# Rescheduling the fill, the transposes and the cluster products of an attention and MLP kernel

## Chip, cores, metric

One NeuronCore of a Trainium2 chip. The metric is the device time of one execution in microseconds, median of the timed runs. "Step" below means one 128-key block of one head; batch 0 to 3 are the four batches of the input, with 48 steps each. SBUF and PSUM are the two memories that this kernel's tiles lie in; M0, M1, M2, OB and SA are PSUM tiles of this kernel. A DMA "lands" when its transfer has ended. Lengths of batches and steps are taken from the start of one exponential to the start of another.

## The reference, cut to what matters

```python
B, H, S, D = 4, 8, 768, 64                      # 16 cluster centroids per head
q_assign = argmax(q_n @ c_n.T); k_assign = argmax(k_n @ c_n.T)
mask   = q_assign[..., :, None] == k_assign[..., None, :]
scores = where(mask, q @ k.T / sqrt(D), -1e9)
attn   = softmax(scores) @ v                    # -> x, 3072 x 512
h = x @ w_in                                    # 512 x 2048
g = h + sin(alpha * h)**2 / (alpha + 1e-9)
out = g @ w_out                                 # 2048 x 512
```

The mask is made by 16 one-hot rows that are appended to the 64 rows of q and k: the score of a query and a key of the same cluster gets a constant more.

## The kernel before

Heads go in pairs (4 pairs a batch). For each pair of batches 0 and 1 (but one) TensorE (PE) transposes q and k in four groups g (`prep_T`, three fp32 transposes each, copied out of PSUM by VectorE, DVE), GpSimd (POOL) casts them into `QK` (`prep_cast`), PE multiplies them with the centroids (`prep_asn`, the "cluster product"), DVE makes the one-hot rows in four pieces (`prep_hot`), and four DMAs bring them into `QK` (`prep_move`). Batches 2 and 3 and the end of batch 1 are transposed by DVE and DMA.

```python
def scores(i):          # 2 matmuls, 512 + 256 columns, into one of two score areas
def expo(i):            # ScalarE (ACT): exp of 128x768
def pv(i):              # 6 matmuls of 65 columns; after the 6th block: rec, xs on DVE
    ...
due = {}                # pv of step r is due at r+3 (first of a head) or r+2
for r in range(ASTEPS):
    due.setdefault(r + (3 if r % NJ == 0 else 2), []).append(r)
    ...
for r in range(ASTEPS):
    i = base + r
    scores(i)
    expo(i)
    ...
    for d in due.get(r, []):
        pv(base + d)
    for fn in plan.get(i, []):     # prep_T, prep_asn, prep_hot ... at their steps
        fn()
    if fill and i not in asn_at:
        fill.go(1)                 # one matmul of the batch before's output
```

So step r%6 = 2 has no PV and step r%6 = 3 has two. The fill matmuls exist in batches 1 to 3: they are the last product (`gT @ w_out`) of the batch before, 64 a batch.

```python
def prep(m, s0):
    if m > 1:
        for g in range(4):
            if m != NHP + 3:
                at(s0 + g, lambda g=g: prep_T(m, g))     # four steps running
        at(s0 + 2, lambda: prep_cast(m, 0))
        at(s0 + 4, lambda: prep_cast(m, 1))
    else:
        s0 -= 4                                          # pair 1: transposed before step 0
    at(s0 + 5, lambda: (prep_asn(m), prep_hot(m, 0)))    # whole product in one step
    at(s0 + 6, lambda: (prep_hot(m, 1), prep_hot(m, 2)))
    at(s0 + 7, lambda: (prep_hot(m, 3), prep_move(m)))
    ...
# --- start, before step 0 (cut) ---
head_asn(0, 0, M0)                 # first cluster product; its one-hot rows gate scores(0)
...
head_move(0, 0, [nc.sync, nc.scalar])
load_v(0); load_qk(2)
prep_T(1, 0, M1, "act"); prep_T(1, 1, M2, "act")
head_asn(0, 1, OB)
...
prep_T(1, 2, M0, "dve"); prep_T(1, 3, M1, "dve")
warmup(4)                          # bf16 matmuls on zeros, result unused
# --- end (cut) ---
spare = [SA[0][:, 0:512], SA[0][:, 512:1024], M1, M2]   # banks of the last output tiles
```

The softmax here doesn't subtract the row's maximum and nothing guards it: scores larger than these inputs give would overflow.

## Time and profile before

| | before |
|---|---|
| timed runs | 320.87, 321.02, 321.75 us; median 321.02 |
| the profiled execution | 323.24 us, span 321.43 us |
| first exponential | 14.30 us |
| first to last exponential, batches 0 to 3 | 42.32, 40.70, 40.34, 38.97 us |
| last exponential to end | 49.23 us |

The page of before; the first line has, for each engine, busy us (share of the span) and number of instructions, the second is the chain that ended last by engine:

```profile
PE 307.7 (96%) x2745; PEld 183.5 (57%) x2787; DVE 207.2 (64%) x362; ACT 242.4 (75%) x326; POOL 112.7 (35%) x174
PE 80%; ACT 6%; DVE 6%; POOL 3%; issue 2%; DMA 1%; SPq 0%; ACTq 0%; DVEq 0%; POOLq 0%
```

PE is what bounds it. Ends of matmuls are modelled, so I read starts. The timeline of before, PE alone, around a step without PV in batch 2 (columns: start us, us, engine, line, operation, out<-in, shape, count):

```profile
173.17 0.38 PE L360 MATMUL M<-w_out_bf,gT 128*128 128x512 bf16 x1
173.38 0.38 PE L313 MATMUL S<-QK 80*128 80x512 bf16 x1
173.60 0.27 PE L314 MATMUL S<-QK 80*128 80x256 bf16 x1
173.71 0.38 PE L360 MATMUL M<-w_out_bf,gT 128*128 128x512 bf16 x1
174.10 0.38 PE L313 MATMUL S<-QK 80*128 80x512 bf16 x1
174.43 0.53 PE L328 MATMUL OB<-VX,pT 128*128 128x65 bf16 x12
174.79 0.38 PE L360 MATMUL M<-w_out_bf,gT 128*128 128x512 bf16 x1
175.02 0.38 PE L313 MATMUL S<-QK 80*128 80x512 bf16 x1
```

A fill matmul (L360) holds PE for 0.21 us (173.17 to 173.38). After the one at 173.71 the next scores start 0.39 us later: 0.18 us are a wait for the exponential that still reads the score area (0.81 us long, from 173.24). In the next step, with two PVs (L328, 12 matmuls) and a fill, PE is late: from scores to scores it takes 0.92 us (174.10 to 175.02).

The end, same view; the bracket is idle time before it and what ended it:

```profile
305.20 1.46 PE L360 MATMUL S<-w_out_bf,gT 128*128 128x512 bf16 x6
307.33 3.61 PE L360 MATMUL S<-w_out_bf,gT 128*128 128x512 bf16 x16 [0.67 <-ACT o_sb L373]
```

And the start, same view:

```profile
12.31 1.41 PE L459 MATMUL S<-warm 128*128 128x512 bf16 x3
13.77 0.38 PE L313 MATMUL S<-QK 80*128 80x512 bf16 x1
13.99 0.27 PE L314 MATMUL S<-QK 80*128 80x256 bf16 x1
```

The warm-ups come about 0.42 us apart, twice the 0.21 of a 512-column matmul later: PE ran at half rate up to about 13.51 us, where the trace's clock record begins. The page's clock row reads full speed there all the same; only the start-to-start times show the half rate. (The record of the fourth warm-up is missing from this trace.)

### The profile page before, as it was taken

What the parts mean: (1) busy time and instruction counts of PE and PEld (TensorE: products, weight loads), DVE (VectorE), ACT (ScalarE), POOL (GpSimd) and SP (SyncE); (2) the same over time, 40 slices, a digit from 0 to 9 for tenths busy, and PEclk for the clock granted to TensorE, in tenths of its full rate; (3) what the DMA queues carried; (4) which work ended last, traced back from release to release, by engine and by line L of the source; (5) the groups of instructions that cost most, each with busy time, mean ns of one, the idle gap of its engine ahead of it and who ended that gap; (6) DMA issues with size and microseconds to landing.
All of it is one profiled execution on the core that took longest, in us unless ns stands there. A gap on an engine that the chain in (4) does not pass through costs nothing.

```text
span 321.4 us, 7151 instructions
## 1 busy us (share of the span) xinstructions
PE 307.7 (96%) x2745; PEld 183.5 (57%) x2787; DVE 207.2 (64%) x362; ACT 242.4 (75%) x326; POOL 112.7 (35%) x174
## 2 busy tenths in 40 slices
PE   7999999899999999999999999999999999999995
PEld 3466665555556565555556566555556666555544
DVE  4488877377858676587858776577835222677721
ACT  5388888787679989687678988777678999687300
POOL 5499788407505363970004476520001000000000
PEclk9999999999999999999999999999999999999999
DMA  6566499996725666881034665420011000000031
GB/s 197 162 199 201 129 191 240 217 204 200 254 89 118 159 150 117 262 297 45 0 98 113 157 164 115 115 82 2 0 67 49 33 2 35 0 36 0 0 133 65
DMA packets 26242, 37.74 MB, mean 117 GB/s; under 512 B 3856, under 2 KB 20064, under 8 KB 26208
## 3 DMA queue, kind: packets, MB, share of 16 engines
q0 software_dynamic: 8704, 19.93, 23.8%
q1 hardware_dynamic: 17264, 17.30, 20.2%
q8 instruction: 22, 0.36, 0.5%
q14 instruction: 12, 0.10, 0.1%
q10 hardware_dynamic: 240, 0.06, 0.1%
HBM read 27.30 MB, written 6.29 MB: 105 GB/s over the span
## 4 chain that ended last, share of the span: by engine, by line
PE 80%; ACT 6%; DVE 6%; POOL 3%; issue 2%; DMA 1%; SPq 0%; ACTq 0%; DVEq 0%; POOLq 0%
PE S L389 16%; PE M L360 16%; PE S L313 13%; PE OB L328 9%; PE M L389 7%; PE S L314 5%; PE OB L360 4%; ACT pT L319 4%; PE M L211 3%; PE S L360 2%; DVE gT L409 2%; PE M L143 2%; POOL QK L185 1%; PE M L352 1%; ACT s_sb L400 1%
## 5 line engine op out<-in xcount | busy, mean ns | idle before, releaser
L319 ACT ACTIVATE pT<-S 128x768 bf16<-128x768 f32 x192 | 145.5, 810 | 23.3 <-PE S L314 19.8
L360 PE MATMUL M<-w_out_bf,gT 128*128 128x512 bf16 (+1 forms) x261 | 83.0, 373 | 0.4 <-DVE gT L409 0.2
L313 PE MATMUL S<-QK 80*128 80x512 bf16 x192 | 73.0, 381 | 4.1 <-ACT pT L319 1.6
L389 PEld LDWEIGHTS <-w_in_bf 128*128 128x128 bf16 x512 | 49.6, 98 | 38.2 <-issue 2.1
L328 PEld LDWEIGHTS <-pT 128*128 128x128 bf16 x1152 | 55.8, 97 | 21.9 <-issue 0.8
L389 PE MATMUL S<-xT,w_in_bf 128*128 128x256 bf16 (+1 forms) x345 | 64.8, 325 | 1.5 <-DVE gT L409 0.8
L328 PE MATMUL OB<-VX,pT 128*128 128x65 bf16 x1152 | 60.7, 194 | 0.6 <-DVE xs L340 0.4
L190 POOL TENSOR_SCALAR QK<-T 64x384 bf16<-64x384 f32 x64 | 33.9, 529 | 69.0 <-DMA T<-Tq 65.8
L400 ACT ACTIVATE s_sb<-S,alpha_col 128x768 bf16<-128x768 f32 x44 | 39.3, 900 | 23.8 <-PE S L389 14.5
L360 PEld LDWEIGHTS <-gT 128*128 128x128 bf16 x400 | 39.0, 98 | 26.3 <-issue 1.5
L314 PE MATMUL S<-QK 80*128 80x256 bf16 x192 | 52.0, 271 | 0.0
L409 DVE SCALAR_TENSOR_TENSOR gT<-u_sb,ralpha,S 128x768 bf16<-128x768 bf16 x44 | 44.5, 1014 | 11.5 <-ACT u_sb L405 8.1
L314 PEld LDWEIGHTS <-QK 80*128 80x128 bf16 x192 | 18.9, 98 | 22.0 <-issue 7.4
L185 POOL CAST QK<-T 64x768 bf16<-64x768 f32 x32 | 26.9, 840 | 8.8 <-DVE T L149 4.0
L389 PE MATMUL M<-xT,w_in_bf 128*128 128x256 bf16 (+1 forms) x154 | 29.4, 324 | 0.3
L339 DVE RECIPROCAL rec<-OB 128x6 f32<-128x6 f32 x32 | 6.2, 194 | 36.2 <-PE OB L328 36.1
L407 DVE TENSOR_TENSOR u_sb<-s_sb 128x768 bf16<-128x768 bf16 x40 | 23.4, 586 | 7.9 <-ACT s_sb L400 7.9
L202 POOL CAST VX<-v 128x768 bf16<-128x768 f32 x16 | 14.2, 889 | 38.4 <-PE OB L328 34.2
L409 DVE SCALAR_TENSOR_TENSOR gT<-u_sb,ralpha,M 128x512 bf16<-128x512 bf16 (+1 forms) x40 | 22.8, 611 | 6.2 <-ACT u_sb L405 5.8
L400 ACT ACTIVATE s_sb<-M,alpha_col 128x512 bf16<-128x512 f32 (+1 forms) x40 | 20.9, 573 | 7.3 <-PE M L389 7.3
L360 PE MATMUL OB<-w_out_bf,gT 128*128 128x512 bf16 (+1 forms) x79 | 25.8, 358 | 0.0
L313 PEld LDWEIGHTS <-QK 80*128 80x128 bf16 x192 | 18.7, 97 | 12.0 <-issue 9.6
(81 smaller groups left out, 272.3 us busy)
## 6 DMA issues: line engine op xcount, KB each, us to landing
T<-Tq SPq DMA_DIRECT2D x64, 96.0 KB, 2.3
out_dram<-o_sb SPq DMA_DIRECT2D x23, 256.0 KB, 2.1
v<-in_v_dram POOLq DMA_DIRECT2D x14, 384.0 KB, 4.9
q<-in_q_dram POOLq DMA_DIRECT2D x13, 384.0 KB, 4.4
k<-in_k_dram POOLq DMA_DIRECT2D x13, 384.0 KB, 5.2
w_in_bf<-in_moe_w_in_dram POOLq DMA_DIRECT2D x4, 512.0 KB, 8.3
w_out_bf<-in_moe_w_out_dram POOLq DMA_DIRECT2D x4, 512.0 KB, 11.5
QK<-ohT SPq DMA_DIRECT2D x60, 24.0 KB, 2.8
```

The costliest lines, as they stand in the source:

```text
L185: nc.gpsimd.tensor_copy(out=QK[0:D, m % NQK, h, :, HS * par : HS * par + HS], in_=src)
L190: nc.gpsimd.tensor_scalar(out=QK[0:D, m % NQK, h, t].rearrange("c (n i a) -> c i n a", i=4, a=32)[:, 2 * par : 2 * par + 2], in0=src[:, t] ...
L202: nc.gpsimd.tensor_copy(out=VX[m % NVX][:, :, :, 0:D], in_=st[m]["v32"])
L313: nc.tensor.matmul(out=dst[:, 0:512], lhsT=lhsT, rhs=T[:, 0, 0:512], start=True, stop=True)
L314: nc.tensor.matmul(out=dst[:, 512:S], lhsT=lhsT, rhs=T[:, 0, 512:S], start=True, stop=True)
L319: nc.scalar.activation(out=pT, in_=area(i)[:, 0:S], func=ACTF.Exp, scale=escale)
L328: nc.tensor.matmul(out=o3[:, j, :], lhsT=pT[:, P * j : P * j + P], rhs=VX[m % NVX][:, h, jof(m // NHP, kt), :], start=(kt == 0 and j == 0) ...
L360: nc.tensor.matmul(out=bk[:, lo:hi], lhsT=gT[:, f, P * mt : P * mt + P], rhs=w_out_bf[:, f, lo:hi], start=(f == 0), stop=(f == NF - 1),)
L389: nc.tensor.matmul(out=ar[lo // 512][:, 0 : hi - lo] if isinstance(ar, tuple) else ar[:, lo:hi], lhsT=lhsT, rhs=xT[:, kk, lo:hi], start=(k ...
L400: nc.scalar.activation(out=s_sb[:, lo:hi], in_=src, func=ACTF.Sin, scale=alpha_col[:, f : f + 1])
L407: nc.vector.tensor_tensor(out=u_sb, in0=s_sb, in1=s_sb, op=ALU.mult)
L409: nc.vector.scalar_tensor_tensor(out=gT[:, f, lo:hi], in0=u_sb[:, lo:hi], scalar=ralpha[:, f : f + 1], in1=src, op0=ALU.mult, op1=ALU.add,)
```

## The change

Its intent: give PE in every step of batches 1 to 3 about the same work; in batch 0, put transposes and halves of the cluster product one per step; start the scores of pair 0 before pair 1's last two transpose groups; warm PE earlier; free the end of its bank wait.

```diff
-    def prep_asn(m, bk=None):
+    def prep_asn(m, part=0, parts=1):          # half of the columns each
 ...
+    load_v(0)                                  # earlier: ahead of load_qk(1)
     load_qk(1)
 ...
+    warmup(2)
     head_asn(0, 0, M0)
 ...
-    prep_T(0, 3, SA[1][:, 0:512], "act")
+    prep_T(0, 3, M1, "act")
 ...
-    prep_T(1, 0, M1, "act")
-    prep_T(1, 1, M2, "act")
+    prep_v(0)
     head_asn(0, 1, OB)
 ...
-    prep_v(0)
-    prep_cast(1, 0)
-    prep_T(1, 2, M0, "dve")
-    prep_T(1, 3, M1, "dve")
-    warmup(4)
-    prep_cast(1, 1)
+    prep_T(1, 0, M2, "act")
+    prep_T(1, 1, M0, "act")
     load_v(1)
+    warmup(2)
 ...
+    def pair_steps(m, make, half, cast):
+        for g, i in make:
+            at(i, lambda g=g: prep_T(m, g))
+        for h in range(2):
+            at(cast[h], lambda h=h: prep_cast(m, h))
+        at(half[0], lambda: prep_asn(m, 0, 2))
+        a = half[1]
+        at(a, lambda: (prep_asn(m, 1, 2), prep_hot(m, 0)))
+        at(a + 1, lambda: (prep_hot(m, 1), prep_hot(m, 2)))
+        at(a + 2, lambda: (prep_hot(m, 3), prep_move(m)))
 ...
-    for m, s0 in {1: 0, 2: 4, 3: 12, 4: 20, 5: 28, 6: 36, 7: ASTEPS + 2}.items():
-        prep(m, s0)
+    for m, make, half, cast in (
+        (1, ((2, 0), (3, 1)), (4, 5), (0, 3)),
+        (2, ((0, 2), (1, 6), (2, 7), (3, 8)), (11, 12), (7, 10)),
+        (3, ((0, 10), (1, 13), (2, 14), (3, 17)), (19, 20), (14, 18)),
+        (4, ((0, 18), (1, 22), (2, 23), (3, 24)), (29, 30), (23, 25)),
+        (5, ((0, 25), (1, 26), (2, 31), (3, 32)), (35, 36), (27, 33)),
+        (6, ((0, 34), (1, 37), (2, 38), (3, 41)), (43, 44), (38, 42)),
+    ):
+        pair_steps(m, make, half, cast)
 ...                                            # loads of q, k at fixed steps; alpha at 42; pair 7 by hot_steps
-            if fill and i not in asn_at:
-                fill.go(1)
+            if fill:
+                fill.go((2 if r % NJ == 2 else 0 if r % NJ == 3 else 1) - (i in asn_at))
 ...
-    spare = [SA[0][:, 0:512], SA[0][:, 512:1024], M1, M2]
+    spare = [SA[0][:, 0:512], M1, SA[0][:, 512:1024], M2]
```

More of the change, by code (lines that the diff above doesn't have):

```diff
@@ L202, in prep_v @@
         nc.gpsimd.tensor_copy(out=VX[m % NVX][:, :, :, 0:D], in_=st[m]["v32"])
-    def prep_asn(m, bk=None):
+    def prep_asn(m, part=0, parts=1):
         s = st[m]
         hp = pair_of[m][1]
-        bk = bank() if bk is None else bk
+        if part == 0:
+            s["asn"] = bank()[:, 0:HS]
+        w = HS // parts
         for g in range(4):
             nc.tensor.matmul(
-                out=bk[32 * g : 32 * g + 32, 0:HS],
+                out=s["asn"][32 * g : 32 * g + 32, w * part : w * part + w],
                 lhsT=cnB[:, 2 * hp + g // 2, :],
-                rhs=s["T32"][:, g, :],
+                rhs=s["T32"][:, g, w * part : w * part + w],
                 start=True,
@@ L217, in prep_asn @@
             )
-        s["asn"] = bk[:, 0:HS]
     def head_asn(m, h, bk):
@@ L497 @@
     prep_T(0, 2, SA[0][:, 0:512], "act")
-    prep_T(0, 3, SA[1][:, 0:512], "act")
+    prep_T(0, 3, M1, "act")
     head_move(0, 0, [nc.sync, nc.scalar])
-    load_v(0)
     load_qk(2)
     prep_cast(0, 1)
-    prep_T(1, 0, M1, "act")
-    prep_T(1, 1, M2, "act")
+    prep_v(0)
     head_asn(0, 1, OB)
@@ L532, in hot_steps @@
         at(a + 3, lambda: (prep_hot(m, 3), prep_move(m)))
-    def prep(m, s0):
-        if m > 1:
-            for g in range(4):
-                if m != NHP + 3:
-                    at(s0 + g, lambda g=g: prep_T(m, g))
-            at(s0 + 2, lambda: prep_cast(m, 0))
-            at(s0 + 4, lambda: prep_cast(m, 1))
-        else:
-            s0 -= 4
-        at(s0 + 5, lambda: (prep_asn(m), prep_hot(m, 0)))
-        at(s0 + 6, lambda: (prep_hot(m, 1), prep_hot(m, 2)))
-        at(s0 + 7, lambda: (prep_hot(m, 3), prep_move(m)))
-        asn_at.add(s0 + 5)
+    def pair_steps(m, make, half, cast):
[8 more added lines that the diff above has]
+        at(a + 2, lambda: (prep_hot(m, 3), prep_move(m)))
     def prep_new(m, k0):
@@ L554, in prep_new @@
         hot_steps(m, k0 + 8)
-    for m, s0 in {1: 0, 2: 4, 3: 12, 4: 20, 5: 28, 6: 36, 7: ASTEPS + 2}.items():
-        prep(m, s0)
-        if m == NHP + 3:
-            at(ASTEPS - 8, lambda m=m: load_qk(m, eng=nc.gpsimd))
-        elif m > 2:
-            at(max(0, s0 - 14), lambda m=m: load_qk(m, eng=nc.gpsimd))
+    for m, make, half, cast in (
[6 rows of a table added]
+    ):
+        pair_steps(m, make, half, cast)
+    for h in range(2):
+        at(ASTEPS + 4 + 2 * h, lambda h=h: prep_cast(NHP + 3, h))
+    hot_steps(NHP + 3, ASTEPS + 7)
+    for m, i in {3: 0, 4: 8, 5: 15, 6: 22, 7: 38}.items():
+        at(i, lambda m=m: load_qk(m, eng=nc.gpsimd))
     late = []
@@ L586, in alpha @@
         nc.vector.reciprocal(out=ralpha, in_=ralpha)
-    at(15, alpha)
+    at(42, alpha)
     def load_w_in(n):
```

## The prediction

> **What bounds the kernel now.** TensorE: the page gives PE 96% busy, ACT 75%, DVE 64%; the chain of waits is 80% PE. Busy PE is modelled, so I read start-to-start times in the timeline. An attention step costs PE 0.32 us of scores, 0.195 of PV (6 matmuls) and, from batch 1 on, 0.21 of a fill matmul. Two score areas alternate: scores of step i+2 wait for the exponential of step i (0.81 us), so two steps take at least 1.45 us.
>
> **Fill (batches 1 to 3).** Six steps without one-hot work take 0.73, 0.73, 0.71, 0.91, 0.73, 0.73 us between exponentials. The step without PV has 0.53 us of PE work, and the next scores wait 0.18 us for the exponential (timeline: fill at 173.71, scores at 174.10). Moving one fill there from the step with two PVs makes 0.75 and 0.71: 0.17 us saved per group. Groups with the cluster product (0.8 us) in the no-PV step don't wait and gain nothing. Free groups: 3 + 3 + 6, plus each batch's first (0.21): 2.7 us, all on the chain.
>
> **End.** The first matmul of output tile 3 waits for ACT's copy out of the other half of its PSUM tile: a PE gap of 0.7 us near 307. Its own bank removes it: -0.75.
>
> **Start.** First exponential at 14.30 us; its one-hot rows landed at 11.6, but PE had pair 1's transposes and 4 warm-ups in front. Two transpose groups leave (1.2 us), and head 1's cluster product no longer waits behind pair 1's loads. Two warm-ups in front of the first cluster product delay it by 0.35. First exponential: about 13.1. [...] Net -0.8.
>
> **Batch 0.** First to last exponential: 42.3 us, against 33 at ACT's 0.707 a step. PE work is about 38: transposes 0.36 a group, product 0.8. The new schedule spreads the lumps (steps of 1.4 to 1.6 us). But it takes in two transpose groups of pair 1 (+0.72 PE, +0.9 DVE), and DVE gets nearly full: 36 us of work in 42. Adding up the PE and DVE queues step by step with the trace's durations (this gives 42.3 for before) shows new waits: pair 1's one-hot ends 9.1 us after the first scores, and its moves (0.62 us issue each, 1.8 to 4.4 to landing) end after step 12 wants them, 1 to 2 us lost; the half product at step 35 waits 1 us for a tile on DVE. So 42.9: +0.6 (-1.5 to +2).
>
> **Sum.** 321.0 - 2.7 - 0.75 - 0.8 + 0.6 = 317.3; leaning slightly lower, since the schedule looks tuned: **317.0 us, range 314.3 to 319.5**. Faster by over 2%: 0.11; within: 0.88; slower: 0.01.
>
> **Right or wrong.** Right if no-PV and two-PV steps read about 0.75/0.71 instead of 0.71/0.91; the gap near 307 is gone; the first exponential comes near 13; steps of 1.4 us mostly leave batch 0, but one is long at 11 to 12 (scores waiting for a DMA of one-hot rows) and one near 35. The stretches between batches (31.6 us) should not change.
>
> **What would make it wrong.** [...]no stall at step 12 (1.5 more gained); DVE backlog stalling more of batch 0; fills in the no-PV step delaying the scores behind them.

The sum came to 317.3 us, and the lean made it 317.0. In the start's paragraph a rule for the clock that no run here shows is cut, and with it the term of +0.4 that rested on it: the -0.8 in the sum is -1.2 (14.30 to 13.1) and that +0.4.

## The result

Ratios below are the mean time of one kernel's runs over that of the other's runs of the same rounds, so not quite the ratio of the medians quoted. Executions over 1.5% slower than the fastest of the same kernel are left out of the means.

| | before | after |
|---|---|---|
| median | 321.38 us (320.87 to 321.83, 4 runs) | 319.31 us (318.93 to 319.74, 4 runs) |
| ratio | | 0.9936 (0.9914 to 0.9959) |
| profiled execution, span | 321.43 us | 317.56 us |
| clock record begins | 13.51 us | 6.42 us |
| first exponential | 14.30 us | 12.27 us |
| batch 0 | 42.32 us | 43.51 us |
| batches 1, 2, 3 | 40.70, 40.34, 38.97 us | 40.34, 39.71, 37.79 us |
| last exponential to end | 49.23 us | 48.39 us |

The median fell by 2.07 us where I had said 4.0. The two traces differ by 3.87, which was the first sign that one of them was not typical. The page of after, as above:

```profile
PE 306.6 (97%) x2835; PEld 183.0 (58%) x2835; DVE 205.3 (65%) x362; ACT 241.3 (76%) x326; POOL 111.3 (35%) x174
PE 86%; DVE 7%; ACT 2%; DMA 2%; issue 1%; SPq 0%; DVEq 0%; ACTq 0%
```

The step without PV, PE's timeline of after:

```profile
171.77 0.38 PE L361 MATMUL M<-w_out_bf,gT 128*128 128x512 bf16 x1
171.98 0.38 PE L314 MATMUL S<-QK 80*128 80x512 bf16 x1
172.20 0.27 PE L315 MATMUL S<-QK 80*128 80x256 bf16 x1
172.31 0.59 PE L361 MATMUL M<-w_out_bf,gT 128*128 128x512 bf16 x2
172.75 0.38 PE L314 MATMUL S<-QK 80*128 80x512 bf16 x1
173.07 0.53 PE L329 MATMUL OB<-VX,pT 128*128 128x65 bf16 x12
173.44 0.38 PE L314 MATMUL S<-QK 80*128 80x512 bf16 x1
```

Two fills take 0.44 us from 172.31 to 172.75 and no wait is left; the step with two PVs goes from scores to scores in 0.69 us (172.75 to 173.44). The no-PV step became 0.76 us between exponentials and the two-PV step 0.71; before they were 0.71 and 0.91. The end, same view: the gap is gone.

```profile
304.76 2.32 PE L361 MATMUL M<-w_out_bf,gT 128*128 128x512 bf16 x10
306.92 3.62 PE L361 MATMUL S<-w_out_bf,gT 128*128 128x512 bf16 x16
```

The start, same view: here the scores wait for a DMA of one-hot rows, and the warm-ups before them run at full rate (0.21 us apart).

```profile
9.77 0.59 PE L461 MATMUL S<-warm 128*128 128x512 bf16 x2
11.75 0.38 PE L314 MATMUL S<-QK 80*128 80x512 bf16 x1 [1.39 <-DMA QK<-ohT]
```

Batch 0 is 1.2 us longer, though its lumps went: nine steps over 1.15 us (up to 1.6) are gone, but three new ones came: step 11 with 2.17 us (before 0.94), step 35 with 2.20 us (before 0.74) and step 2 with 1.23 us (before 0.71). These are PE's waits in batch 0 of after (12 to 56 us: us in total, times, longest us; the first line contains the wait of the start):

```profile
PE S L314 <- DMA QK<-ohT: 2.4, 2, 1.4
PE M L213 <- DVE T L149: 0.6, 1, 0.6
PE M L143 <- DMA q<-in_q_dram: 0.4, 1, 0.4
PE OB L329 <- DVE xs L341: 0.2, 1, 0.2
```

Step 11, PE's timeline of after: after the half product of pair 2 PE idles until pair 1's one-hot rows land, planned at step 7 and due at step 12.

```profile
22.16 0.53 PE L213 MATMUL M<-T,cnB 128*32 128x192 f32 x8
23.72 0.38 PE L314 MATMUL S<-QK 80*128 80x512 bf16 x1 [1.03 <-DMA QK<-ohT]
```

Step 35, PE and then DVE in the timeline of after. The product of pair 5 needs all four transposed tiles; the last copy (T, the first of the two in the last line, ended at 45.38) stands in DVE's queue behind one-hot work of pair 4 (oh, ohT).

```profile
44.30 0.53 PE L213 MATMUL M<-T,cnB 128*32 128x192 f32 x6
45.44 0.51 PE L213 MATMUL M<-T,cnB 128*32 128x192 f32 x2 [0.61 <-DVE T L149]
```

```profile
42.51 1.08 DVE L256 TENSOR_TENSOR oh<-asT,amax 128x384 bf16<-128x384 f32 x1
43.51 0.55 DVE L149 TENSOR_SCALAR T<-M 128x384 f32<-128x384 f32 x1
43.98 0.96 DVE L273 STREAM_TRANSPOSE ohT<-oh 128x768 bf16<-128x768 bf16 x1
44.87 0.98 DVE L149 TENSOR_SCALAR T<-M 128x384 f32<-128x384 f32 x2
```

### The profile page after: what moved, and what is told of

Same layout as the page of the kernel before. It is cut to its first block, busy times and chain, and to the rows that moved or that the text cites. A ratio compares the mean times of both kernels' runs of the same rounds, so it can differ in the third digit from the quotient of the medians.

```text
span 317.6 us, 7292 instructions
## 1 busy us (share of the span) xinstructions
PE 306.6 (97%) x2835; PEld 183.0 (58%) x2835; DVE 205.3 (65%) x362; ACT 241.3 (76%) x326; POOL 111.3 (35%) x174
## 4 chain that ended last, share of the span: by engine, by line
PE 86%; DVE 7%; ACT 2%; DMA 2%; issue 1%; SPq 0%; DVEq 0%; ACTq 0%
PE M L361 18%; PE S L390 16%; PE S L314 12%; PE OB L329 10%; PE M L390 8%; PE S L315 6%; PE OB L361 5%; PE M L213 4%; PE S L361 2%; DVE gT L410 2%; PE M L143 2%; PE M L353 1%; ACT s_sb L401 1%; DMA q<-in_q_dram 1%; DVE u_sb L408 1%
## 5 line engine op out<-in xcount | busy, mean ns | idle before, releaser
L361 PE MATMUL M<-w_out_bf,gT 128*128 128x512 bf16 (+1 forms) x288 | 90.7, 373 | 0.3 <-DVE gT L410 0.3
L390 PE MATMUL S<-xT,w_in_bf 128*128 128x512 bf16 x352 | 65.2, 326 | 1.0 <-DVE gT L410 0.8
L390 PE MATMUL M<-xT,w_in_bf 128*128 128x512 bf16 (+1 forms) x160 | 29.9, 326 | 0.0
L202 POOL CAST VX<-v 128x768 bf16<-128x768 f32 x16 | 13.5, 844 | 34.3 <-PE OB L329 33.4
```

The lines of the kernel that those rows point to most:

```text
L202: nc.gpsimd.tensor_copy(out=VX[m % NVX][:, :, :, 0:D], in_=st[m]["v32"])
L361: nc.tensor.matmul(out=bk[:, lo:hi], lhsT=gT[:, f, P * mt : P * mt + P], rhs=w_out_bf[:, f, lo:hi], start=(f == 0), stop=(f == NF - 1),)
L390: nc.tensor.matmul(out=ar[lo // 512][:, 0 : hi - lo] if isinstance(ar, tuple) else ar[:, lo:hi], lhsT=lhsT, rhs=xT[:, kk, lo:hi], start=(k ...
```

## The experiments

Sixteen kernels ran, in four groups; each group shared eleven runs of before on its chip (medians 321.66, 321.44, 321.44 and 321.33 us). All results were correct.

### 1. Is the profile of before typical? (before_again, before_third)

No edit. Theory A: the profiled execution was one with a late clock; rival B: its start is typical.

> The kernel before, unchanged. Theory A: the profiled execution of before was not typical: its clock was granted only at 13.5 us (after: 6.4 us), its whole run took 323.2 us where the timed ones took 320.9 to 321.8, and so its first exponential at 14.30 us overstates what the start can give. A expects a profile with the grant at another time, first exponential 12.3 to 13.3 us and span 319 to 320, or a spread of timed runs of over 0.8 us. Rival B: the 14.30 us start is typical and the change lost the missing 1.7 us in the timed runs somewhere else; B expects 14.2 to 14.4 again and a span of 321 to 321.8.

> The kernel before once more: a third sample of its start. Theory: grant anywhere from 4.5 to 13.5 us; first exponential 12.0 to 12.5 unless the grant is later than 11; timed median 321.2 to 321.7 with one run in ten at 323 or more.

| kernel, start code | clock record begins | first exponential |
|---|---|---|
| before | 13.51 | 14.30 |
| before_again | 9.52 | 12.50 |
| before_third | 4.68 | 11.91 |
| fill_only (start of before) | 4.71 | 11.97 |
| end_only (start of before) | 4.57 | 11.99 |

Five executions of the same start code span 2.4 us in the first exponential. before_again took 321.45 us (321.14 to 322.86, ratio 1.0006) with a span of 319.59; before_third 321.09 us (ratio 0.9987). The timeline of PE in before_again shows what differs: the warm-ups come 0.216 us apart, not 0.42.

```profile
11.11 1.03 PE L459 MATMUL S<-warm 128*128 128x512 bf16 x4
11.97 0.38 PE L313 MATMUL S<-QK 80*128 80x512 bf16 x1
12.19 0.27 PE L314 MATMUL S<-QK 80*128 80x256 bf16 x1
```

Theory A stands: 14.30 us was not typical. Of 59 timed runs of before four took over 322.5 us; the profile that I predicted from (323.24) belongs to that tail. Against before_again the sum closes: start 12.50 to 12.27 (-0.23), batch 0 +1.34, batches 1 to 3 -0.38, -0.66, -1.12, the stretches between them -0.14, end -0.84: -2.03 in the spans, -2.07 in the medians.

### 2. The parts one by one (fill_only, end_only, start_only)

fill_only is before with this edit alone:

```diff
-            if fill and i not in asn_at:
-                fill.go(1)
+            if fill:
+                fill.go((2 if r % NJ == 2 else 0 if r % NJ == 3 else 1) - (i in asn_at))
```

> Before with the fill rule alone. The comparison of the two traces gives -0.36, -0.63 and -1.18 us in batches 1, 2 and 3: -2.2 in all (ratio 0.993). My prediction had -2.7. If the fill's part interacts with the rest of the change it will differ from -2.2 by over 0.5.

Measured 319.45 us, ratio 0.9942 (0.9921 to 0.9962). In its trace the three batches are 0.64, 0.63 and 1.15 us shorter than in before_again: 2.4 us (batch 0 of that execution was 0.9 us longer, see 4). In the changed kernel it is 2.16. The difference lies in batch 1, where the product of pair 7 now draws another PSUM bank: in step 8 the second fill starts a new output tile in the bank that this product still holds. That step takes 0.98 us there and 0.76 in fill_only. (The bank is read from the program's order and from the times; no run was made for it. But transposes_back, below, differs from after_both only in two transposes, which come earlier and name their bank, so that two draws fewer come before pair 7's: there step 8 fell from 0.97 to 0.76 us.)

end_only is before with the new order of `spare` alone.

> Before with the order of the last output tiles' banks alone. Theory: the PE gap near 307 us goes, -0.75 us (ratio 0.9977). Rival: the gap is filled by the store of the last tile and nothing is gained.

Measured 320.12 us, ratio 0.9956 (0.9944 to 0.9968). Its trace has 48.38 us from the last exponential to the end against 49.23: 0.85 us. The timed gain, 1.4, is larger than that; no trace shows where the surplus of 0.5 us lies; it may be the spread of starts. The rival fell.

start_only is before with the start of after, pair 1's two transpose groups at steps 0 and 1 and, because they come later, its casts at 0 and 3 and its whole product at step 3:

```diff
+    load_v(0)                      # ahead of load_qk(1)
+    warmup(2)                      # ahead of head_asn(0, 0, M0)
 ...                                # transposes, casts, warm-ups as in after
-            s0 -= 4
+            s0 -= 2
+            at(0, lambda: (prep_T(1, 2), prep_cast(1, 0)))
+            at(1, lambda: prep_T(1, 3))
+            at(3, lambda: prep_cast(1, 1))
```

> Before with the start of the changed kernel alone: its prologue, pair 1's two transposes behind pair 0's scores, and pair 1's cluster product two steps later; steps, fill and end as before. My prediction had -0.8 us for the start (first exponential 13.1 against 14.30), besides the +0.72 of transposes that enter batch 0. Theory now: with an early grant both starts wait for the landing of the first one-hot rows, so the first exponential stays at 11.9 to 12.5, and the loop takes the two transposes: total +0.3 to +1.2 us (ratio 1.001 to 1.004). By the prediction's reading of the start: -0.1 us or less, ratio up to 1.000.

Measured 322.06 us, ratio 1.0011 (0.9984 to 1.0038): the theory's range, but the interval holds 1.000 too. The trace decides more: first exponential 11.75 us, inside the range of before's starts, and batch 0 takes 43.66 us, 1.5 more than before_again. The start alone brings nothing and costs the loop something.

### 3. The clock at the start (early_warm_before, no_warmups_before, no_warmups_after, after_no_early_warmups)

```diff
# early_warm_before: before, with
+    warmup(2)
     head_asn(0, 0, M0)
# no_warmups_before, no_warmups_after: in warmup()
-        for _ in range(n):
+        for _ in range(0):
# after_no_early_warmups: after, with
-    warmup(2)
     head_asn(0, 0, M0)
```

> Before with two more warm-up matmuls in front of the first cluster product, nothing else. Theory C: these two matmuls bring the full clock earlier (grant near 6.4 us as in the profile of after) and the start shortens by 0.5 to 1.5 us. Rival D: the time of the grant is chance and the warm-ups only delay the first one-hot by up to 0.35 us; the total is unchanged or up to 0.4 us longer.

321.95 us, ratio 1.0017 (0.9997 to 1.0036); clock record from 5.12 us, first exponential 12.33. The whole was not shortened: rival D's range for the time, theory C's for the clock.

> The kernel before with all warm-up matmuls taken out (they compute nothing that is used). Theory A: the time of the clock grant, not the order of PE's work, made the first exponential 14.30 us in the profile of before. Without warm-ups the grant should come late in most executions (10 us or later), the first exponential at 13 us or later and the whole 1 to 2.5 us longer in the timed runs. Rival B: PE's queue of pair 1's transposes and four warm-ups sets 14.30; without the warm-ups (0.9 to 1.7 us of PE in front) the first exponential comes earlier than 13.4 us even with a late grant.

322.28 us, ratio 1.0018 (0.9984 to 1.0052), not told apart from before. Record from 11.01, first exponential 12.24: rival B's number. Theory A's did not come: the first exponential is not at 13 us or later, and the whole is not shown to be longer. This fits a queue of transposes and warm-ups at half rate as the maker of 14.30: in that trace PE worked with no gap over 0.12 us from 8.3 us to the scores at 13.77, 2.1 us after the landing of the one-hot rows (11.64). But the clock was 2.5 us earlier here, so the run does not separate the late clock from the queue; the start of 14.30 had both. The later batch 0 (43.91 us) has long steps at 1 and 11.

> The changed kernel with no warm-ups at all, for comparison with no_warmups_before (322.3 us median, first exponential 12.24, grant 11.0). Theory: with a late grant too the first exponential waits for the first one-hot rows, so it stays at 12.0 to 12.6 and the change gains the same 2 us (319.5 to 320.5). By the prediction's reading (PE's queue in front of the scores) it would be 0.7 us or more before that of no_warmups_before, 11.5 or less.

319.16 us, ratio 0.9935 (0.9910 to 0.9960), record from 9.98. The two starts without warm-ups, PE's timeline, first of no_warmups_before, then of no_warmups_after:

```profile
11.04 0.49 PE L143 MATMUL M<-ident_f,k 128*128 128x128 f32 x3
11.72 0.38 PE L313 MATMUL S<-QK 80*128 80x512 bf16 x1 [0.19 <-DMA QK<-ohT]
```

```profile
10.11 0.49 PE L143 MATMUL M<-ident_f,k 128*128 128x128 f32 x3
11.68 0.38 PE L314 MATMUL S<-QK 80*128 80x512 bf16 x1 [1.08 <-DMA QK<-ohT]
```

The work that the change takes out of the way becomes a wait for the same DMA (0.19 becomes 1.08 us), and the scores start within 0.04 us of each other. This is where the start's expected gain went.

> The changed kernel without the two warm-ups in front of the first cluster product. So far the nine profiles of kernels with these two have the grant at 4.7 to 7.0 us; of four profiles with the prologue of before two have it late (9.5 and 13.5). Theory: the two warm-ups make the early grant likely, and that is what they are worth: without them the grant is at 9 us or later in the profile or the timed runs spread over 1.5 us, mean up to 1 us longer than the changed kernel (319.2). Rival: chance; the same time or 0.3 us less.

318.87 us, ratio 0.9920 (0.9902 to 0.9939): not slower than the changed kernel (0.9936 and 0.9924), so the early warm-ups are not shown to be worth anything. The clock record began at 9.89 us. In the ten profiles of kernels that have them it began at 4.3 to 7.0 us; in the eight without, at 4.6 to 13.5 with five at 9.5 or later. That the warm-ups bring the clock early is not shown by this, since the kernels differ in other ways. This profile also fell into another kind of slow execution (322.18 us against 318.5 to 319.0 of the rest): the clock went back to half from 26.96 to 30.37 us, a stretch of 3.41 us.

The traces show what PE did before the clock came. Cut backwards from the start of the clock record into stretches of 3.41 us, the length just seen, before reads (stretch, length, busy us and count of PE, PEld, DVE, ACT, POOL, the clock row, the DMA share and GB/s):

```profile
3.27:6.68 3.41, 2.85 (x16) 1.55 (x15) 1.72 (x9) 2.21 (x4) 1.02 (x4) 1.00 0.91 277
6.68:10.10 3.42, 3.23 (x16) 2.03 (x12) 1.73 (x5) 1.45 (x4) 1.94 (x3) 1.00 0.21 78
10.10:13.51 3.41, 3.41 (x18) 1.93 (x18) 2.22 (x7) 0.87 (x2) 0.43 (x1) 1.00 0.69 197
```

In all 18 traces PE was busy for 2.99 to 3.41 us of the last stretch (3.31 or more in 16), and in none of an earlier one for more than 3.23. What brings the clock is not shown: busy is modelled, no edit tested it, and 2.99 was followed by the clock in after_m1_early, 3.23 was not in before.

### 4. The two new waits (after_again, after_m1_early, after_m5_late, after_both)

```diff
# after_m1_early
-        (1, ((2, 0), (3, 1)), (4, 5), (0, 3)),
+        (1, ((2, 0), (3, 1)), (2, 3), (0, 3)),
# after_m5_late
-        (5, ((0, 25), (1, 26), (2, 31), (3, 32)), (35, 36), (27, 33)),
+        (5, ((0, 25), (1, 26), (2, 31), (3, 32)), (37, 38), (27, 33)),
# after_both: both; after_again: neither
```

> The changed kernel, unchanged, so that the next three are compared with it on the same chip. Ratio to before 0.9936 again (0.992 to 0.995). In the profile: long steps of about 2.2 us at steps 11 and 35 of batch 0, and 43 to 43.6 us from first to last exponential of batch 0.

319.25 us, ratio 0.9924; steps 11 and 35 take 2.17 us each, batch 0 43.42 us, as expected.

> The changed kernel with pair 1's half cluster products (and with them its one-hot and moves) two steps earlier. Theory: the long step 11 (2.17 us) is the wait of pair 1's scores for its one-hot rows, which are planned too late. Expected: that step back to about 0.9 us, batch 0 shorter by 1.0 us (0.6 to 1.3), ratio to the changed kernel 0.997. Rival: the scores wait for the casts of GpSimd or the wait only moves to another step of DVE's queue: under 0.3 us gained.

318.03 us, ratio 0.9893. Step 11 fell from 2.17 to 1.08 us and batch 0 from 43.42 to 42.31: 1.11 us, and 1.09 in the mean of the timed runs (319.13 to 318.04). The wait was pair 1's one-hot rows; the rival fell.

> The changed kernel with pair 5's half cluster products two steps later (its scores come only in step 60). Theory: the long step 35 (2.2 us) is PE in order, held at a half product whose last transposed tile DVE has not yet copied. Expected: 0.7 us less in batch 0 (0.3 to 1.2), ratio 0.998. Rival: DVE is full, the wait moves to steps 37 to 45: under 0.2 us gained.

318.48 us (317.94 to 323.60; the five fast runs 317.94 to 320.04), ratio 0.9907. The profile is not compared in time. Its windows view shows the half clock in it (columns as above):

```profile
10.40:13.82 3.42, 1.96 (x13) 1.17 (x12) 1.48 (x4) 2.19 (x5) 3.10 (x5) 1.00 0.57 172
13.82:24.06 10.24, 9.98 (x75) 6.46 (x76) 4.31 (x9) 4.86 (x7) 3.94 (x5) 0.50 0.44 145
24.06:34.00 9.94, 8.45 (x121) 6.28 (x120) 6.06 (x13) 7.66 (x10) 5.87 (x8) 1.00 0.43 130
```

PE was busy 1.96 of 3.42 us, then had half the clock for 10.24 us; in after_no_early_warmups it was busy 1.42 of the 3.41 us before the half clock. Whether PE's idle time brought it is not shown: in after_again PE was busy 1.83 us from 8.44 to 11.85, the second 3.41 us after its clock record began, and the clock stayed. Step 35 itself fell to 0.71 us.

> Both of these. Theory: DVE has room, the two waits add up: batch 0 takes 41.3 to 42 us and the whole 1.7 us less than the changed kernel (ratio to before 0.988). Rival: DVE's total work bounds batch 0: under 1.2 us for both.

317.68 us, ratio 0.9888 (0.9856 to 0.9921); batch 0 41.60 us, 1.8 less than after_again and 0.7 less than after_m1_early, so in the traces the two waits add up. PE's waits in batch 0 (12 to 54 us) of after_both are now one line:

```profile
PE S L314 <- ACT pT L320: 0.4, 2, 0.2
```

The timed median gained 1.6 us against after_again, with one run of 320.01 in six. With that run the mean gains 1.1, inside the rival's range (under 1.2), and equals that of after_m1_early (317.99 and 318.04): that pair 5's wait is worth another 0.7 us is shown by the traces, not by the timed runs.

A side finding on DVE: fill_only and end_only have the same batch 0, yet step 21 took 1.85 us in one and 1.25 in the other (1.60 in before). The timeline of end_only, the one-hot comparison on DVE and the cast on POOL:

```profile
29.23 0.60 DVE L255 TENSOR_TENSOR oh<-asT,amax 128x384 bf16<-128x384 f32 x1
29.45 1.06 POOL L185 CAST QK<-T 64x768 bf16<-64x768 f32 x1
```

And of fill_only:

```profile
29.44 1.20 DVE L255 TENSOR_TENSOR oh<-asT,amax 128x384 bf16<-128x384 f32 x1
29.40 0.82 POOL L185 CAST QK<-T 64x768 bf16<-64x768 f32 x1
```

In these two traces the one that started first took about its usual time (0.60 and 0.82 us) and the other longer (1.06 and 1.20), which the profile shows as busy time, not as a wait. (In end_only an earlier cast, from 28.60 us, still ran for 0.2 us beside the comparison; spans on POOL are rough.) In fill_only PE then waits 0.65 us for DVE before its next PV. The comparison takes 0.56 us with POOL idle (in after at 18.55), the cast 0.82 (median of 32 in before). What holds the later one is not shown.

### 5. A faster kernel (transposes_back, best_mix, best_second)

```diff
# transposes_back: after_both, with
     prep_T(1, 1, M0, "act")
+    prep_T(1, 2, M1, "dve")
+    prep_T(1, 3, M2, "dve")
 ...
-        (1, ((2, 0), (3, 1)), (2, 3), (0, 3)),
+        (1, (), (2, 3), (0, 3)),
# best_second: transposes_back, with pair 2's first transpose at step 5 in place of 2
# best_mix: transposes_back, with
+        (1, (), (1, 2), (0, 3)),
+        (2, ((0, 4), (1, 6), (2, 7), (3, 8)), (11, 12), (7, 9)),
+        (3, ((0, 9), (1, 10), (2, 13), (3, 14)), (19, 20), (11, 15)),
+        (4, ((0, 17), (1, 22), (2, 24), (3, 25)), (29, 30), (23, 26)),
+        (5, ((0, 26), (1, 27), (2, 31), (3, 32)), (37, 38), (28, 33)),
+        (6, ((0, 34), (1, 36), (2, 37), (3, 38)), (42, 43), (37, 39)),
+    hot_steps(NHP + 3, ASTEPS + 8)
```

> after_both (changed kernel, pair 1's product earlier, pair 5's later) with pair 1's last two transpose groups put back in front of the first scores. Theory: there they run while PE waits for the one-hot rows and cost nothing: first exponential unchanged within 0.3 us, batch 0 0.7 us shorter (41.6 to 40.9), ratio to before near 0.986. Rival: they delay the first scores by 0.7 us or more and nothing is gained.

316.66 us (316.33 to 316.97), ratio 0.9837 (0.9812 to 0.9862): the fastest kernel by this ratio, 4.8 us under the median of before. First exponential 12.23 (after_both 11.89, after 12.27); the rows landed 0.34 us later than in after_both (11.57 against 11.23), and the scores followed 0.14 us after in both, so the transposes did not delay them. Batch 0 took 41.24 against 41.60: 0.4 of the 0.7 us expected, all in step 2 (1.62 to 1.25). Another 0.2 came from step 8 of batch 1 (see 2). The spans differ by only 0.3 us, the timed medians by 1.0, and the intervals of the two ratios overlap, so the size of the gain is open.

> What the experiments point to: transposes_back, with pair 2's first transpose moved behind its load (step 2 waits about 0.5 to 0.9 us for a DMA), the transposes of pairs 3 to 6 at steps that the one-hot work leaves free, and the product of pair 7 one step later (the step of 0.98 us in batch 1 becomes 0.76). Theory: batch 0 takes 39 to 40.5 us, first exponential 11.9 to 12.5, the whole 1 to 2 us less than transposes_back, 315 to 316.5 us timed (ratio 0.980 to 0.984). Rival: DVE[...] cannot follow: 41 us or more for batch 0.

A miss: 317.68 us, ratio 0.9867, slower than transposes_back. Batch 0 took 41.32 us, the rival's number but not by its cause: PE's longest wait there, 0.75 us, was for a load, because k of pair 3 landed only at 20.59 us and its transpose, moved to step 10, waited for it (that step took 1.78 us). Batch 1 took 41.09 us, 1.0 more: pair 7's product in step 8 waited for the PSUM bank of a fill tile, 0.94 us until DVE had copied that tile out.

> transposes_back with pair 2's first transpose at step 5 in place of 2, so that PE does not wait for its load. Theory: step 2 of 1.25 us becomes 0.75 to 0.9 and no later step grows by as much: 0.3 to 0.7 us less than transposes_back (316.66), ratio to before 0.982. Rival: step 3 (1.26) keeps the wait, because the loads of pair 2 or v land late anyway: within 0.2 us.

316.80 us (4 runs), ratio 0.9858, span 314.69 against 314.84: a tie, and the rival's range. Step 2 fell from 1.25 to 0.88 us, and step 9 grew from 0.74 to 1.08. The wait for the load was real, but removing it gave nothing.

## Why the prediction was half right

| term | predicted | traces, after against before_again |
|---|---|---|
| start | -0.8 | -0.23 (and +0.36 against before_third) |
| batch 0 | +0.6 | +1.34 |
| fill, batches 1 to 3 | -2.7 | -2.16 |
| end | -0.75 | -0.84 |
| stretches between batches | 0 | -0.14 |
| lean for "looks tuned" | -0.35 | |
| whole | -4.0 | -2.03 (medians -2.07) |

The measured time lies inside the range, and the class (within 2%) was right, but the gain is half of what was forecast.

- **End.** Right in cause and size; end_only shows it by itself.
- **Fill.** Right in cause; the step times 0.76/0.71 against 0.75/0.71 predicted. The size was 0.5 too large: the twelve free groups gained 0.16 us each, not 0.17; the eight groups with the product, which I let gain nothing, lost about 0.01 each; and the bank collision in batch 1 cost 0.22 more. fill_only, without that collision, has 2.4.
- **Batch 0.** Both waits that I named came, at the steps that I named, and after_m1_early and after_both took them away. The term was mis-sized by 0.7: +1.34 measured. The sum left out that pair 2's first transpose, moved to step 2, would wait for its load (PE waits 0.4 us for q there; that step took 1.23 us instead of 0.71). Whether this accounts for the 0.7 is not shown: best_second took that wait away from transposes_back and batch 0 did not get shorter. For pair 1's two transposes I counted 0.72 us of PE; start_only, which moves them and pair 1's product, has a batch 0 that is 1.5 us longer. My range of -1.5 to +2 held it.
- **Start.** This is the step that failed in kind: "First exponential: about 13.1", from 14.30. The 14.30 belonged to one execution of 323.24 us, and I subtracted its repair from a median of other executions. In typical ones the start of before was 11.9 to 12.5 us, and that of after 11.9 to 12.3, not 13.1. What failed is the path: I had PE's queue in front of the first scores, as in that execution, where they came 2.13 us after the last of the first one-hot rows landed. In before_again and before_third they came 0.43 and 0.32 us after it, in after 0.13. So PE's queue had only 0.2 to 0.3 us to give (an estimate from these differences); beyond that, the change replaced PE work by waiting for DMA. no_warmups_before and no_warmups_after (12.24 and 12.20) show it directly. An execution of after with the clock as late as 13.5 us was never caught, so what the change does there is open.
- **The lean** of 0.35 us had no measurement behind it and pointed the wrong way.

What of the change paid, then, in the traces: the fill and the end, 3.0 us. Moving pair 1's transposes into the loop and the new batch 0 schedule took 1.3 back.

## What to carry to other kernels

Before costing a stage from a profile, set the profiled execution's time beside the timed median; if they differ by as much as the gain in question, profile the same kernel again and see which stage moved. Work in front of a DMA wait was free here: taking it away turned it into idle time (0.19 us of waiting became 1.08), and in a loop that PE bounds it costs something (putting two transposes back took 0.4 us off batch 0), so ask of each move what its old place waited for. Evening out PE's work between steps paid nearly the wait that the traced step showed (0.16 of 0.18 us), as long as the extra work does not land on a buffer that is still in use (where it did, in one step of batch 1, that step took 0.98 us instead of 0.76).
